# Row tiles for every projection: two 64-row array tiles that take turns on two PSUM banks, in a fixed instruction order, with x held in SBUF

## The chip, the cores, the metric

One core of a Trainium2 chip runs the whole program. The metric is the device time of one execution in microseconds; medians of several executions are given. A profiled execution has a *span* (first to last instruction); the measured time is 1.7 to 2.1 us longer than the span here.

## The reference

A transformer block of 2048 tokens and width 576: layer norm, linear attention with 32 heads of 18, and a gated GELU network of width 4608, both on the normalized x, both added to x. All data are bf16.

```python
def reference(x, wqkv, wo, w_gate, w_up, w_down):          # cut to what matters
    xn = layernorm(x)                                      # 2048 x 576
    q, k, v = split_heads(xn @ wqkv)                       # 32 heads of 18
    phi = lambda t: where(t > 0, t + 1, exp(t)) + 1e-6
    pq, pk = phi(q), phi(k)
    kv, z = einsum(pk, v), sum_over_tokens(pk)
    o = (pq @ kv) / (pq . z + 1e-6)
    return x + o @ wo + (gelu(xn @ w_gate) * (xn @ w_up)) @ w_down
```

The width 576 is 4 x 128 + 64. Each projection therefore contracts over four full chunks of 128 rows and one chunk of 64 rows; what to do with the half chunk is the subject of the change.

## The kernel before

The stages follow each other: for each tile of 128 tokens layer norm, transposes and the K and V projections with the products of phi(K) and V ("K/V stage"); then Q; then, four times (for 512 tokens each), gate/up followed by the down projection. TensorE's products go to *PSUM tiles* of one bank here and two in the changed kernel, which are reused in turn: a product waits until the last reader of its tile is done. Three engines work on phi: ScalarE makes relu(-t) and then exp, VectorE max(t, 0) + eps, GpSimd adds the two. phi_e and phi_a are the buffers between them. The *denominators* are the products pq . z (`ps_den`).

```python
    def phi(ps_ap, out_ap, rows, cols, add_eng):
        e = awork.tile([P, SC], F32, name="phi_e", tag="phi_e")
        nc.scalar.activation(out=e[...], in_=ps_ap, func=ACT.Relu, scale=-1.0)
        nc.scalar.activation(out=e[...], in_=e[...], func=ACT.Exp, scale=-1.0)
        a = awork.tile([P, SC], F32, name="phi_a", tag="phi_a")
        nc.vector.tensor_scalar(out=a[...], in0=ps_ap, scalar1=0.0, scalar2=EPS_ATT, op0=ALU.max, op1=ALU.add)
        add_eng.tensor_tensor(out=out_ap, in0=e[...], in1=a[...], op=ALU.add)

    # K, V, Q: five full-array products per output; the fifth chunk of the weights is padded with zeros
            for kt in range(KT):
                nc.tensor.matmul(ps_k[:, :HALF], lhsT=xnT[:, kt, ts_], rhs=wqkv_sb[:, kt, ...],
                                 start=(kt == 0), stop=(kt == KT - 1))

    # gate and up: four full-array products each, then the two half chunks as one pair of 64-row tiles
        def full(self, first):
            ...
                        nc.tensor.matmul(pst[:], lhsT=wsb[:, kt, fcol], rhs=xnT[:, kt, self.cs], ...)
        def pairs(self, first):
            for i in range(self.r):
                nc.tensor.matmul(self.g[i][:], lhsT=self.wr[0:64, fcol], rhs=xnT[0:64, 4, self.cs], ...)
                nc.tensor.matmul(self.u[i][:], lhsT=self.wr[64:128, fcol], rhs=xnT[64:128, 4, self.cs], ...)
    # ... two batches in a row, the second in the order pairs, full: one change of tiling mode in, one out
    # ... denominators of the first 512 tokens: in the first five double batches of gate/up
    # ... Q: every third add of phi on VectorE, the others on GpSimd
    # ... each down tile loads its x again for the last addition
```

The order of instructions on each engine was left to a scheduler.

## Time and profile before

The time was 544.41 us (median of 3). Read from the timeline of TensorE:

| | before |
|---|---|
| first K matmul | 10.94 us |
| K of two tiles to K of the next two | 6.02 us |
| Q starts | 63.22 |
| gate/up starts (from Q's start) | 84.82 (21.60) |
| gate/up stages, from first to last slot | 74.49, then three of 71.85; sum 290.04 |
| span | 542.6 |

A *slot* is the time from one start on TensorE to the next. With 512 columns it is 216 ns, whether one full-array product or two 64-row products side by side fill it. In the page, "PE 528.8 (97%)" is time in which TensorE had work; it does not say that each slot did as much as it could.

### The profile page before, as it was taken

The numbers are of one execution on the slowest core, as the hardware profiler recorded it, in microseconds if no ns is written. First come the engines' busy times: TensorE is split into PE (matmuls) and PEld (weight loads), VectorE is DVE, ScalarE is ACT, GpSimd is POOL, SyncE is SP. The second block draws the span as 40 slices with busy tenths as digits, with TensorE's granted clock in tenths as the row PEclk, the third lists the DMA queues.
The fourth block names the chain that finished last, engine by engine and source line by source line (L and its number), as shares of the span: only waits on it lengthen the run. The fifth ranks groups of instructions, "written<-read, shape, count | busy, mean of one in ns | idle before, by whom it ended". The sixth has DMA issues, their size and how long they took to land.

```text
span 542.6 us, 8817 instructions
## 1 busy us (share of the span) xinstructions
PE 528.8 (97%) x3371; PEld 311.4 (57%) x3403; DVE 258.0 (48%) x462; ACT 152.0 (28%) x329; POOL 67.8 (12%) x79
## 2 busy tenths in 40 slices
PE   5999999999999999999999999999999999999997
PEld 4788764444457774444477744444677644445775
DVE  5996598877248613333288123323683123323101
ACT  3677797223330003223200013223100122322000
POOL 1445465101002100000011000000021000000000
PEclk8999999999999999999999999999999999999999
DMA  8920003897840114554511035545301245540000
GB/s 251 251 78 2 1 2 95 254 257 211 227 135 24 29 34 141 155 145 143 163 52 38 28 103 145 161 137 154 110 23 32 74 136 157 148 127 0 23 18 16
DMA packets 104851, 58.08 MB, mean 107 GB/s; under 512 B 5802, under 2 KB 104746, under 8 KB 104810
## 3 DMA queue, kind: packets, MB, share of 16 engines
q1 hardware_dynamic: 104810, 57.53, 37.6%
q8 instruction: 26, 0.43, 0.4%
q14 instruction: 15, 0.12, 0.1%
HBM read 55.15 MB, written 2.36 MB: 106 GB/s over the span
## 4 chain that ended last, share of the span: by engine, by line
PE 92%; DMA 2%; DVE 2%; SPq 1%; issue 1%; POOL 0%; ACT 0%; POOLq 0%; ACTq 0%
PE acc L468 26%; PE g L392 23%; PE u L392 23%; PE g L400 6%; PE ps_q L332 4%; PE acc L475 4%; DMA xg<-in_A_x_dram 2%; PE ps_k L242 2%; PE ps_v L256 2%; PE ps_den L365 1%; DVE stats L216 1%; DVE phi_a L206 1%; SPq L150 0%; PE tp_x L233 0%; DVE xn L223 0%
## 5 line engine op out<-in xcount | busy, mean ns | idle before, releaser
L409 DVE TENSOR_TENSOR hT<-u,gl 128x512 bf16<-128x512 f32 x144 | 95.7, 686 | 171.9 <-PE u L402 104.2
L408 ACT ACTIVATE gl<-g 128x512 f32<-128x512 f32 x144 | 81.9, 596 | 321.3 <-PE u L402 262.2
L468 PE MATMUL acc<-wd_sb,hT 128*128 128x288 bf16 x1152 | 146.4, 286 | 0.0
L468 PEld LDWEIGHTS <-hT 128*128 128x128 bf16 x1152 | 112.6, 98 | 30.0
L370 DVE RECIPROCAL den_sb<-den_sb 126x128 f32<-126x128 f32 (+3 forms) x100 | 68.0, 746 | 0.7
L371 POOL TENSOR_TENSOR pqT<-pqT,den_sb 126x512 bf16<-126x512 bf16 (+1 forms) x20 | 23.2, 1161 | 298.4 <-DVE den_sb L370 298.4
L480 DVE TENSOR_TENSOR res<-acc,xres 128x288 bf16<-128x288 f32 x32 | 14.6, 457 | 88.3 <-PE acc L475 88.3
L392 PE MATMUL u<-xnT,wu_133 128*128 128x512 bf16 x144 | 37.0, 379 | 0.1
L392 PE MATMUL u<-xnT,wu_131 128*128 128x512 bf16 x144 | 37.0, 379 | 0.1
L392 PE MATMUL u<-xnT,wu_130 128*128 128x512 bf16 x140 | 36.6, 379 | 0.3
L392 PE MATMUL g<-xnT,wg_128 128*128 128x512 bf16 x139 | 36.5, 379 | 0.2
L392 PE MATMUL g<-xnT,wg_127 128*128 128x512 bf16 x136 | 36.0, 380 | 0.7 <-issue 0.5
L392 PE MATMUL u<-xnT,wu_132 128*128 128x512 bf16 x140 | 36.4, 379 | 0.2
L392 PE MATMUL g<-xnT,wg_129 128*128 128x512 bf16 x137 | 36.1, 380 | 0.5 <-issue 0.3
L392 PE MATMUL g<-xnT,wg_126 128*128 128x512 bf16 x140 | 36.4, 379 | 0.1
L242 PE MATMUL ps_k<-wqkv_sb,xnT 128*128 128x288 bf16 x160 | 24.4, 304 | 6.0 <-DVE xnT L234 5.7
L204 ACT ACTIVATE phi_e<-phi_e 128x288 f32<-128x288 f32 (+2 forms) x52 | 26.7, 514 | 1.5
L475 PE MATMUL acc<-m_sb,pqT 126*128 126x288 bf16 (+1 forms) x160 | 24.9, 285 | 0.0
L392 PEld LDWEIGHTS <-wg_127 128*128 128x128 bf16 x144 | 12.6, 98 | 20.7 <-issue 7.9
L392 PEld LDWEIGHTS <-wg_129 128*128 128x128 bf16 x144 | 12.6, 98 | 20.4 <-issue 7.6
L392 PEld LDWEIGHTS <-wu_130 128*128 128x128 bf16 x144 | 14.1, 98 | 17.0
L392 PEld LDWEIGHTS <-wu_131 128*128 128x128 bf16 x144 | 14.1, 98 | 17.0
(96 smaller groups left out, 504.6 us busy)
## 6 DMA issues: line engine op xcount, KB each, us to landing
wd_sb<-in_B_w_down_dram SPq DMA_DIRECT2D x12, 432.0 KB, 4.0
wg_126<-in_B_w_gate_dram SPq DMA_DIRECT2D x18, 256.0 KB, 3.0
wu_130<-in_B_w_up_dram SPq DMA_DIRECT2D x18, 256.0 KB, 4.0
wg_127<-in_B_w_gate_dram SPq DMA_DIRECT2D x18, 256.0 KB, 3.0
wu_131<-in_B_w_up_dram SPq DMA_DIRECT2D x18, 256.0 KB, 3.3
wg_128<-in_B_w_gate_dram SPq DMA_DIRECT2D x18, 256.0 KB, 3.0
wu_132<-in_B_w_up_dram SPq DMA_DIRECT2D x18, 256.0 KB, 3.5
wg_129<-in_B_w_gate_dram SPq DMA_DIRECT2D x18, 256.0 KB, 3.1
```

The lines of the kernel that those rows point to most:

```text
L204: nc.scalar.activation(out=e[:rows, :cols], in_=e[:rows, :cols], func=ACT.Exp, scale=-1.0)
L242: nc.tensor.matmul(ps_k[:, :HALF], lhsT=xnT[:, kt, ts_], rhs=wqkv_sb[:, kt, D + hf * HALF: D + (hf + 1) * HALF], start=(kt == 0), stop=(kt ...
L332: nc.tensor.matmul(ps[:rows, :], lhsT=wqkv_sb[:, kt, q0:q0 + rows], rhs=xnT[:, kt, sc * SC:(sc + 1) * SC], start=(kt == 0), stop=(kt == KT ...
L370: nc.vector.reciprocal(out=dsb[:rows, q * w:(q + 1) * w], in_=dsb[:rows, q * w:(q + 1) * w])
L371: nc.gpsimd.tensor_tensor(out=pqT[:rows, c, cs], in0=pqT[:rows, c, cs], in1=dsb[:rows, :], op=ALU.mult)
L392: nc.tensor.matmul(pst[:], lhsT=wsb[:, kt, fcol], rhs=xnT[:, kt, self.cs], start=(first and kt == 0), stop=(not first and kt == 3),)
L400: nc.tensor.matmul(self.g[i][:], lhsT=self.wr[0:64, fcol], rhs=xnT[0:64, 4, self.cs], start=first, stop=not first)
L408: nc.scalar.activation(out=gl[:], in_=self.g[i][:], func=ACT.Gelu_apprx_tanh)
L409: nc.vector.tensor_tensor(out=hT[:, self.f0 + i, :], in0=self.u[i][:], in1=gl[:], op=ALU.mult)
L468: nc.tensor.matmul(a_ps[:, :HALF], lhsT=hT[:, f, j * P:(j + 1) * P], rhs=wd_sb[:, f, hf * HALF:(hf + 1) * HALF], start=(f == 0), stop=False,)
L475: nc.tensor.matmul(a_ps[:, :HALF], lhsT=pqT[:rows, c, ts_], rhs=m_sb[:rows, c, hf * HALF:(hf + 1) * HALF], start=False, stop=(c == NCH - 1),)
L480: nc.vector.tensor_tensor(out=res[:, hf * HALF:(hf + 1) * HALF], in0=a_ps[:, :HALF], in1=xres[:, hf * HALF:(hf + 1) * HALF], op=ALU.add,)
```

## The change

The intent: where 64-row products go in pairs, a slot holds two halves of anything, so the 18 half chunks of two outputs fill nine slots without padding and without changing the tiling mode. The kernel never lets two row tiles write one bank at the same time (the rule that the prediction cites), so the low rows begin with output 0 and the high rows with output 1 (first phase, five slots), and then they trade banks (second phase, four slots). Between the phases each must know that the other has finished with the bank: an empty instruction on SyncE's queue waits for the end of the first phase, and the second phase waits for it. In the diff this is the *turn*.

```diff
+        def p1(self):
+            for kt in (4, 0, 1, 2, 3):
+                self.mm(0, LO, kt, kt == 4, False)
+                last = self.mm(1, HI, kt, kt == 4, False)
+            self.turn = nc.sync.nop()
+            tc.add_manual_dep(self.turn.ins, last.ins.name, SYNC, reason="the row tiles take turns on a bank")
+
+        def p2(self):
+            for kt in range(4):
+                m = self.mm(1, LO, kt, False, kt == 3)
+                if kt == 0:
+                    tc.add_manual_dep(m.ins, self.turn.ins.name, SYNC, reason="the bank's other row tile has written")
+                self.mm(0, HI, kt, False, kt == 3)
...   K, V, Q, gate and up all use these units; the zero padding goes
+    ctx.enter_context(tc.manual_schedule())
+    x_sb = persist.tile([P, NS, D], BF16, name="x_sb")
...   phi on two banks at once (576 or 1024 columns), all adds on GpSimd:
+            e = awork.tile([P, 2 * SC], F32, name="phi_e", tag="phi_e", bufs=3)
+            a = awork.tile([P, 2 * SC], F32, name="phi_a", tag="phi_a", bufs=2)
...   one round of the K/V stage, in program order:
+        if more:
+            ln_norm(n + 2)
+            ln_norm(n + 3)
+        ka, kb = project_pair(n, "k")
+        fa, fb = k_phi(n, ka), k_phi(n + 1, kb)
+        fa.read()
+        fb.read()
+        if more:
+            tp = transposes([n + 2, n + 3])
+            tp_copy(tp, 0, n + 2, nc.vector.tensor_copy)
+            tp_copy(tp, 1, n + 3, nc.scalar.copy)
...
+        fa.finish()
+        fb.finish()
...
+        va, vb = project_pair(n, "v")
...   the denominators of the first 512 tokens move ahead of gate/up:
+    kv_stage2()
+    den0 = [(c_, den_mm(0, c_)) for c_ in ([0, 1], [2, 3], [4])]
...
-            nc.sync.dma_start(xres[:], x_view[:, n, :])
```

## The prediction

> **What bounds the kernel now.** I read the page first (busy shares, chain of waits), then what TensorE waits for, then its timeline inside the gate/up stage, then the groups of the engines beside it.
>
> ```profile
> span 542.6 us, 8817 instructions
> PE 528.8 (97%) x3371; PEld 311.4 (57%) x3403; DVE 258.0 (48%) x462; ACT 152.0 (28%) x329; POOL 67.8 (12%) x79
> PE 92%; DMA 2%; DVE 2%; SPq 1%; issue 1%; POOL 0%; ACT 0%; POOLq 0%; ACTq 0%
> ```
>
> TensorE is busy 97% and carries 92% of the chain that ended last. So only two things can win time: fewer TensorE slots, or the 14 us in which it idles. The view of waits says where it idles:
>
> ```profile
> PE warm L96 <- POOL ident masks.py:199: 1.8, 1, 1.8
> PE ps_k L242 <- DVE xnT L234: 5.7, 2, 4.4
> ```
>
> The idle time is the start: the first K matmul starts at 10.94 us (timeline), 4.4 us of it because VectorE computed the statistics of tiles 2 and 3, whose load landed at 7.94, before it copied the transposes of tiles 0 and 1. Next the timeline of TensorE in the gate/up stage:
>
> ```profile
> 203.47 1.03 PE L392 MATMUL u<-xnT,wu_132 128*128 128x512 bf16 x4
> 204.42 0.39 PE L400 MATMUL g<-xnT,wr_136 64*128 64x512 bf16 x1
> 204.43 0.39 PE L402 MATMUL u<-xnT,wr_136 64*128 64x512 bf16 x1
> 204.65 0.38 PE L400 MATMUL g<-xnT,wr_136 64*128 64x512 bf16 x1
> 204.87 0.38 PE L400 MATMUL g<-xnT,wr_137 64*128 64x512 bf16 x1
> 205.08 0.38 PE L400 MATMUL g<-xnT,wr_137 64*128 64x512 bf16 x1
> 205.39 1.04 PE L392 MATMUL g<-xnT,wg_129 128*128 128x512 bf16 x4
> ```
>
> Starts are what count here. Full-array matmuls of 512 columns start every 216 ns, those of 288 columns every 122 ns (medians of the starts). The 64-row pairs start together, 3 ns apart, and the next pair follows after 216: two half matmuls cost one slot. But into the pairs it takes 312 ns and out again 312, and the first pair takes 227: 96 + 96 + 11 = 203 ns lost, in each of 36 double batches.
>
> **What the Trainium skill says.**
> - "TensorEngine Tiling (Array Packing)", Key Properties: changing the tiling mode drains TensorE, changing the tile does not. The trace agrees: the 203 ns above.
> - The same page, Gotcha 1: two row tiles may not use one PSUM bank at once, and software must see to it. Nothing in the trace before shows it (g and u pairs have their own banks); it is why the new kernel needs a wait at each change of turns.
> - "SBUF — State Buffer", Who interferes with whom: VectorE in a 2-port mode and GpSimd lock each other out for a whole instruction. The trace agrees: the 64-column normalization takes 0.29 us alone and 0.78 beside GpSimd, and once the 576-column one took 0.78 instead of 0.42.
>
> ```profile
> 20.60 0.29 DVE L227 TENSOR_SCALAR xn<-xg,mv,rstd 128x64 bf16<-128x64 bf16 x1
> 21.93 1.67 POOL L209 TENSOR_TENSOR pk_171<-phi_e,phi_a 128x288 bf16<-128x288 f32 x2 [3.48 <-DVE mv L218]
> 22.85 0.78 DVE L227 TENSOR_SCALAR xn<-xg,mv,rstd 128x64 bf16<-128x64 bf16 x1
> ```
>
> **The change, part by part.** I go through the stages in order.
>
> *Start.* Statistics, normalization, transposes and copy of tile 0 now come before anything of tile 2. First tile landed at about 3.3 us (3.08 before; now the K weights load beside it): two statistics, aggregate, two small activations, normalization, transposes, copy, then the same for tile 1 (durations 0.43, 0.2, 0.29 + 0.2, 0.43, 0.5, 0.45) give the first K matmul at about 7, the second tile's at 8.8, the first K pair done near 10.3, and the norms of tiles 2 and 3 at 11.9. Gain on the start alone about 3 us.
>
> *K/V stage.* Before: two tiles take 6.02 us (K of one tile starts 3.01 after the last), all of it TensorE. TensorE's part falls: 36 slots of 122 ns instead of 40, plus 0.56 transposes and 0.56 for the kv products, plus two mode changes, makes 5.7. But the order is now fixed, and I find a longer loop through the other engines. From phi's max on VectorE, times worked out by scaling the rows before to the new widths (VectorE 288 to 512 columns: 449 to 682 ns, so 576: 0.75, next start after 0.68; ScalarE relu 402 to 587, so 0.64; exp 0.68):
> two max instructions 1.36; first xnT copy 0.48; then the second xnT copy, on ScalarE, which in the built program waits for VectorE's copy of the same PSUM tile, 0.65; the first exp behind it in ScalarE's queue, 0.68: 3.2 us. Then GpSimd adds twice 576 columns:
>
> ```profile
> L209 POOL TENSOR_TENSOR pqT<-phi_e,phi_a 126x512 bf16<-126x512 f32 x11 | 13.8, 1271 | 9.6 <-DVE phi_a L206 4.4 <-ACT phi_e L204 3.9 <-ACT phi_e L203 1.3
> L209 POOL TENSOR_TENSOR pk_171<-phi_e,phi_a 128x288 bf16<-128x288 f32 x8 | 6.3, 795 | 7.6 <-DVE mv L218 4.9 <-DVE phi_a L206 2.7
> ```
>
> (1271 - 795) / 224 = 2.12 ns a column, so 1.40 each, until 6.0. Meanwhile ScalarE does exp, a V copy, Ln, Exp, so the rstd is there at 4.95. Norm, copy, norm, copy need 1.5: without the lock the next max starts at 6.45, with the lock they end about 1.3 after GpSimd, at 7.3. Either is over 6.02, so this stage becomes slower although TensorE has less to do. With 7.3: norms of tiles 14 and 15 at 11.9 + 6 x 7.3 = 55.7. After that come the rest of its group and the last K pair (6.1), then 4.95 until GpSimd has made the last pk and the last kv product ran. The Q stage starts at 66.7 (lock) or 61.6 (no lock), against 63.2 before.
>
> *Q stage.* TensorE: 10 units of 9 slots, 19.4 us instead of 21.6. But before, every third add was on VectorE; now all are on GpSimd: 1024 columns at 2.12 ns and the same fixed part, 2.35 us a unit against 1.94 of TensorE. phi_a has two buffers, so the max of unit i waits for the add of unit i-2. First add at 5.4, max of unit 9 done at 25.4. The three denominator products, now placed before gate/up, take the PSUM tiles of units 7, 8 and 9: TensorE waits at each and reaches gate/up 25.8 us after the start of Q. Without these waits it would be 20.9: 4.9 us lost. Gate/up so starts at 92.5 (lock) or 87.4, against 84.8 before.
>
> *Gate/up and down.* 144 units of 9 slots of 216 are 279.9 us, as before (8 full slots and one pair each). 36 x 203 ns = 7.3 go; 4 entries and exits, 0.8, come. Turn waits: TensorE to SyncE and back I put at 0.15 to 0.25 us (measured: matmul end to other engines 37 to 107 ns, back to TensorE 55); at 512 columns another unit's 864 or 1080 ns lie between, at 288 columns 490, of which 164 go for the matmul's own end. All hidden. SyncE also issues two loads per unit (0.38 + 0.55 before) but those come ahead of the turn's end. Five denominator products and the transposes (1.4 us) have moved ahead of this stage. The m products now open the first down stage, some 0.3 us of waiting. Down: 1312 slots of 122.5 ns, untouched, as is the tail of 3.3.
> Sum from gate/up's start to the end: 279.9 + 0.8 + 1.5 (m) + 3.3 (denominators) + 160.8 + 3.3 = 449.6, and 0.7 that the same sum misses of the 457.8 before: 450.3.
>
> *x in SBUF.* Removes 16 loads of 147 KB; none was on the chain there. Nothing.
>
> **Sum.** With the lock 92.5 + 450.3 = 542.8 of span; without 537.7. The measured time is 1.8 above the span (544.4 against 542.6): 544.6 or 539.5. I weigh the lock two to one: 543.
>
> **Rivals.**
> 1. The loops don't bite: the K/V stage runs at TensorE's 5.75 us per pair and the Q stage hands over without waiting. Then Q starts near 57, gate/up at 78: span about 528, time 530. For it: the intent is plain, and the start and the 6.5 us of mode changes are real. Against it: the fixed order and the buffer counts, read from the program's own waits, and GpSimd's rate, which is measured.
> 2. A long run in 64-row mode doesn't hold 216 ns a slot. Only four pairs in a row were seen; now 36 instructions go into 1944 ns. Each 5 ns more is 1296 x 5 = 6.5 us, to 550. Against it: full 288-column slots issue two instructions every 122 ns, and 133-column ones every 58 (kv products), so issue is no limit at 54 ns, and the weight loads of the next pair started right with the matmuls of the one before.
> 3. SyncE's queue delays the turns: while w_down loads, a turn's end stands behind loads that wait for their own slots. Then TensorE would lose some tenths per block in the first 18 blocks: 2 to 5 us.
>
> **Range and chances.** The two stages with side loops are worth up to 13 us against the best case, and I am less sure of the K/V loop (a few tenths per group times 7) than of GpSimd's backlog in Q. To be faster by over 2% (533.5) both must be mostly wrong: 0.15. Slower by over 2% (555.3) needs rival 2 or 3 at size: 0.05. Range 533 to 551.
>
> **What would show it.** Right: no gap of 312 ns within a gate/up stage, pairs every 216; K pairs 6.5 to 7.5 us apart with VectorE's norms stretched under GpSimd's adds; GpSimd's 1024-column adds back to back at 2.3 us; TensorE waiting some 5 us in all for VectorE's phi_a ahead of the denominator products; gate/up starting later than 84.8. Wrong: K pairs under 6 us apart (loop or lock misread), Q to gate/up within 22 us (adds faster than 2 us), slots of 220 or more, or waits of TensorE for SyncE.

## The result

The changed kernel took 548.3 us (548.06 to 549.0, 4 runs) against 544.47 for the kernel before (544.19 to 545.38, 4 runs): ratio 1.007, 95% interval 1.0056 to 1.0084. By the interval it is a little slower. All outputs are right. The page of the changed kernel:

```profile
span 546.8 us, 11385 instructions
PE 527.7 (97%) x4891; PEld 310.7 (57%) x4891; DVE 247.4 (45%) x378; ACT 148.7 (27%) x247; POOL 71.9 (13%) x66
PEclk8999997999999999999999999999999999999999
PE 82%; DVE 5%; ACT 4%; POOL 3%; issue 3%; SPq 2%; DMA 1%; ACTq 0%; DVEq 0%; POOLq 0%
```

TensorE is still busy 97%, but in the chain of waits it fell from 92% to 82%: VectorE, ScalarE and GpSimd now carry 12% where they carried 2%. The third line is the granted clock in 40 slices: a 7 in the seventh slice (82 to 96 us) stands out. The view of what TensorE waits for (total us, number of times, longest):

```profile
PE tp_x L276 <- DVE xn L264: 4.9, 4, 1.4
PE ps_den L481 <- DVE phi_a L235: 4.1, 3, 1.7
PE ps_k L204 <- ACT v L301: 1.9, 5, 0.4
PE gu L204 <- SPq L213: 0.9, 6, 0.2
```

Before, the only large entry was K waiting at the start. Now there are transposes that wait for a norm, the denominator products that wait for VectorE's phi_a, K products that wait for ScalarE's copy of V, and gate/up products that wait for SyncE. The starts by stage, from the timeline of TensorE:

| | before | after | difference to before, cumulative |
|---|---|---|---|
| first K matmul | 10.94 | 8.85 | -2.1 |
| K pair to K pair | 6.02 | 6.81 | |
| Q starts | 63.22 | 64.60 | +1.4 |
| gate/up starts (from Q's start) | 84.82 (21.60) | 90.86 (26.26) | +6.0 |
| four gate/up stages | 290.04 | 285.32 (72.52, 70.70, 70.99, 71.11) | |
| span | 542.6 | 546.8 | +4.1 |

So the time came in at two places ahead of gate/up, and gate/up gave back less than its mode changes were worth. Each of the three places can be seen.

*A round of the K/V stage in the changed kernel*, from the timeline of all engines (start us, duration us, engine, line, operation; in brackets the idle time before it and what ended that):

```profile
43.44 2.77 POOL L241 TENSOR_TENSOR pk<-phi_e,phi_a 128x576 bf16<-128x576 f32 x2 [4.04 <-ACT phi_e L240]
43.84 0.63 ACT L301 CAST v<-ps_v 128x576 bf16<-128x576 f32 x1
44.52 1.77 PE L204 MATMUL ps_k<-wqkv_sb,xnT 64*128 64x288 bf16 x26 [0.39 <-ACT v L301]
44.69 0.20 ACT L260 ACTIVATE rstd<-rstd 128x2 f32<-128x2 f32 x1
44.93 1.45 DVE L264 TENSOR_SCALAR xn<-x_sb,mv,rstd 128x576 bf16<-128x576 bf16 x1 [0.98 <-ACT rstd L260]
46.51 0.42 DVE L264 TENSOR_SCALAR xn<-x_sb,mv,rstd 128x576 bf16<-128x576 bf16 x1
47.06 1.42 DVE L235 TENSOR_SCALAR phi_a<-ps_k 128x576 f32<-128x576 f32 x2
...
48.39 0.48 DVE L280 COPY xnT<-tp_x 128x640 bf16<-128x640 bf16 x1
48.90 0.69 ACT L280 COPY xnT<-tp_x 128x640 bf16<-128x640 bf16 x1 [1.82 <-DVE xnT L280]
49.49 1.26 ACT L240 ACTIVATE phi_e<-phi_e 128x576 f32<-128x576 f32 x2
```

The same norm takes 1.45 us at 44.93 and 0.42 at 46.51. GpSimd's two adds run from 43.44 to 46.21; the long norm ends at 46.38, 0.17 later. Then follow max, VectorE's copy, ScalarE's copy (which waited 1.82 us for VectorE's), and only then the two exps, which hold back the next adds and the next copy of V.

*From Q to gate/up in the changed kernel*, the timeline of TensorE:

```profile
85.71 0.59 PE L481 MATMUL ps_den<-pqT,zrep 126*126 126x512 bf16 x2 [1.06 <-DVE phi_a L235]
88.03 1.01 PE L481 MATMUL ps_den<-pqT,zrep 126*126 126x512 bf16 x2 [1.73 <-DVE phi_a L235]
90.34 0.59 PE L481 MATMUL ps_den<-pqT,zrep 72*72 72x512 bf16 x1 [1.30 <-DVE phi_a L235]
90.86 0.61 PE L204 MATMUL gu<-xnT,wr 64*128 64x512 bf16 x2
91.26 0.63 PE L204 MATMUL gu<-xnT,wg 64*128 64x512 bf16 x1
91.69 0.63 PE L204 MATMUL gu<-xnT,wg 64*128 64x512 bf16 x1
```

Three waits, and then gate/up begins with starts 427 ns apart instead of 216: the array was at half clock. In gate/up that lasts for nine slots. The trace's record of the granted clock falls from 1.0 to 0.5 at 87.8 us, inside the second wait, and rises again at 94.6: the products at 88.03 are slow already (1.01 us for two, 0.59 at 85.71).

*The first block of a gate/up stage in the changed kernel*, the timeline of all engines again:

```profile
319.77 0.33 SPq L574 DMA_DIRECT2D out_dram<-res  x1
...
321.89 0.51 SPq L168 DMA_DIRECT2D wr<-in_B_w_up_dram  x1
321.98 0.38 PE L204 MATMUL gu<-xnT,wg 64*128 64x512 bf16 x1
322.51 0.39 PE L204 MATMUL gu<-xnT,wu 64*128 64x512 bf16 x1 [0.15 <-SPq L213]
```

The second phase of the block's second unit starts 531 ns after the slot before it instead of 216 (that of the first unit, at 321.32, was 482 after). In SyncE's queue the store of the last output and four load issues stood in front of the turn; the last issue ended at 322.40, and the turn came 0.1 after it. In most later blocks the slots are 216 apart; in this stage one more pair of such waits follows, at 372.27 and 373.46, after a load issue of 1.53 us.

### The profile page after: what moved, and what is told of

Its sections match the earlier page's. It is cut to its first block, busy times and chain, and to the rows that moved or that the text cites. A ratio compares the mean times of both kernels' runs of the same rounds, so it can differ in the third digit from the quotient of the medians.

```text
span 546.8 us, 11385 instructions
## 1 busy us (share of the span) xinstructions
PE 527.7 (97%) x4891; PEld 310.7 (57%) x4891; DVE 247.4 (45%) x378; ACT 148.7 (27%) x247; POOL 71.9 (13%) x66
## 3 DMA queue, kind: packets, MB, share of 16 engines
HBM read 52.86 MB, written 2.36 MB: 101 GB/s over the span
## 4 chain that ended last, share of the span: by engine, by line
PE 82%; DVE 5%; ACT 4%; POOL 3%; issue 3%; SPq 2%; DMA 1%; ACTq 0%; DVEq 0%; POOLq 0%
PE gu L204 50%; PE acc L557 26%; PE acc L563 4%; POOL pqT L241 2%; DVE xn L264 2%; ACT phi_e L240 2%; DVE phi_a L235 1%; PE ps_k L204 1%; ACT xnT L280 1%; DMA x_sb<-in_A_x_dram 1%; PE ps_den L481 1%; ACT v L301 1%; SPq L165 1%; PE ps_q L204 1%; SPq L167 1%
## 5 line engine op out<-in xcount | busy, mean ns | idle before, releaser
L204 PE MATMUL gu<-xnT,wu 64*128 64x512 bf16 x1152 | 275.3, 378 | 1.4 <-SPq L213 0.9
L204 PE MATMUL gu<-xnT,wg 64*128 64x512 bf16 x1152 | 275.7, 378 | 0.0
L543 DVE TENSOR_TENSOR hT<-gu,gl 128x512 bf16<-128x512 f32 x144 | 99.5, 691 | 170.3 <-ACT gl L542 170.3
L542 ACT ACTIVATE gl<-gu 128x512 f32<-128x512 f32 x144 | 86.0, 597 | 322.4 <-PE gu L204 300.5
L204 PEld LDWEIGHTS <-wu 64*128 64x128 bf16 x1152 | 107.3, 94 | 73.6 <-SPq L213 9.7
L204 PEld LDWEIGHTS <-wg 64*128 64x128 bf16 x1152 | 107.3, 94 | 69.0 <-issue 2.0
L493 DVE RECIPROCAL den_sb<-den_sb 126x128 f32<-126x128 f32 (+1 forms) x80 | 67.5, 906 | 0.3
L494 POOL TENSOR_TENSOR pqT<-pqT,den_sb 126x512 bf16<-126x512 bf16 (+3 forms) x25 | 24.1, 965 | 299.5 <-DVE den_sb L493 299.5
L204 PE MATMUL gu<-xnT,wr 64*128 64x512 bf16 x288 | 55.1, 380 | 0.0
L204 PEld LDWEIGHTS <-xnT 64*128 64x128 bf16 x576 | 28.9, 96 | 10.3 <-issue 2.9
```

Of the source, the lines that this page charges most:

```text
L204: return nc.tensor.matmul(self.outs[i], lhsT=self.lhs(i, rows, kt), rhs=self.rhs(i, rows, kt), start=start, stop=stop, skip_group_check=True,)
L493: nc.vector.reciprocal(out=d[:, h:h + P], in_=d[:, h:h + P])
L494: nc.gpsimd.tensor_tensor(out=pqT[:rows, c, cols], in0=pqT[:rows, c, cols], in1=d, op=ALU.mult)
L542: nc.scalar.activation(out=gl[:], in_=ps[:, 0, :], func=ACT.Gelu_apprx_tanh)
L543: nc.vector.tensor_tensor(out=hT[:, GUB * k + i, :], in0=ps[:, 1, :], in1=gl[:], op=ALU.mult)
```

## The experiments

The theory: the products in row tiles cost what was foreseen, and the time is lost in three waits that the new fixed order makes: (1) in the K/V stage a loop through VectorE, ScalarE and GpSimd, lengthened by a lock between VectorE's norm and GpSimd's add; (2) ahead of gate/up an in-order wait for PSUM tiles behind GpSimd's backlog; (3) turns behind other work in SyncE's queue. The main rival: the tiling itself costs something, in slots or in turns. Ratios below are to the kernel before; the changed kernel has 1.007 (548.3 us).

| run | ratio to before (95% interval) | median us | before in the same rounds |
|---|---|---|---|
| e1 adds held, 3 buffers | 1.0094 (1.0066 to 1.0122) | 550.48 | 544.81 |
| e2 exps first | 0.9917 (0.9889 to 0.9945) | 540.57 | 544.81 |
| e3 denominators late | 0.9955 (0.9927 to 0.9982) | 542.78 | 544.81 |
| e4 turns on ScalarE | 0.9996 (0.9973 to 1.0019) | 544.87 | 544.81 |
| e5 adds held, 4 buffers | 1.0006 (0.9981 to 1.0031) | 544.59 | 544.57 |
| e6 gate/up as before | 1.0128 (1.01 to 1.0157) | 551.11 | 544.57 |
| e7 a third phi_a | 1.0044 (1.0018 to 1.0069) | 546.75 | 544.57 |
| e8 all three | 0.9779 (0.975 to 0.9808) | 532.64 | 544.57 |
| e9 K/V on the full array | 1.0079 (1.006 to 1.0098) | 548.18 | 543.96 |
| e10 x loaded again | 1.0081 (1.0066 to 1.0096) | 548.37 | 543.96 |
| e11 e8 and a quicker start | 0.9778 (0.9763 to 0.9792) | 531.77 | 543.96 |
| e12 e1 once more | one run | 549.92 | 543.96 |

### e1 and e12: adds held until the norms are done, three buffers

```diff
         if more:
             ln_norm(n + 2)
-            ln_norm(n + 3)
+            normed = ln_norm(n + 3)
+            for f in held:
+                f.add(normed)        # GpSimd's adds of the last group wait for this norm
...
-            a = awork.tile([P, 2 * SC], F32, name="phi_a", tag="phi_a", bufs=2)
+            ...                      # every third one in a buffer of the denominators, so three in all
```

> The K/V loop alone: GpSimd's two adds of a group are held until VectorE has normalized the next two tiles (phi_a gets a third buffer), so that no add runs beside a norm; nothing else moves. Changed kernel: K pairs start 6.81 us apart, the first norm of a group takes 1.45 us, Q starts at 64.60. Theory A (the lock between the norm and GpSimd's add stretches the loop by 1.03 us per group): norms all 0.42, K pairs 5.75 to 5.95 apart, Q starts at 57.5 to 59, time 541 to 542.5. Rival B (the norm is late because rstd or x or ScalarE is late; the lock only fills a gap): K pairs stay within 6.6 to 6.9, time 547.5 to 549.

Its timed runs took 550.1 to 550.5 us, 2 us more than the changed kernel: neither theory's number. Its profiled execution took 1112 us, and the page of e1 shows why it can't serve:

```profile
span 1110.5 us, 11362 instructions
L204 PE MATMUL gu<-xnT,wg 64*128 64x512 bf16 x1152 | 568.7, 677 | 0.0
```

A gate/up product takes 677 ns instead of 378 throughout, and most of the slots are 440 ns instead of 216, while ScalarE's gelu takes its usual 598 (597 in the changed kernel): TensorE alone was at half speed, from start to end (two times 546 would be 1093). So the run was repeated.

> The first try of held adds once more, for one profile at full clock, since the first one ran at half clock throughout. It took 550.5 in the three other runs, 2 us more than the changed kernel, although no norm can run beside an add in it. Theory A (three buffers: the second relu and max of a group wait until the held add has freed theirs, which puts GpSimd into the loop): norms 0.42, a wait of ScalarE or VectorE for GpSimd in each group, K pairs 6.9 to 7.2. Rival B (something outside the K/V stage): K pairs under 6.6 and the loss elsewhere.

In the second profile (549.92 us, beside 550.1 to 550.5 of e1's timed runs) the norms take 0.43 us each, so the lock is gone, but K pairs are 7.49 to 7.52 us apart, and the view of TensorE's waits of e12 has a new first entry:

```profile
PE ps_v L204 <- DVE phi_a L241: 5.4, 5, 1.5
```

Products of V wait for a PSUM tile that VectorE's max has not read yet. Why it has not is in the timeline of e12, a round of it:

```profile
48.82 2.77 POOL L253 TENSOR_TENSOR pk<-phi_e,phi_a 128x576 bf16<-128x576 f32 x2 [4.76 <-PE ps_k L204]
...
50.27 0.65 ACT L240 ACTIVATE phi_e<-ps_k 128x576 f32<-128x576 f32 x1 [1.19 <-POOL pk L253]
50.95 0.76 DVE L241 TENSOR_SCALAR phi_a<-ps_k 128x576 f32<-128x576 f32 x1 [1.09 <-ACT phi_e L240]
```

The second relu waits 1.19 us for the first held add, whose buffer it takes, and the max comes after the relu. Theory A of this run holds, with a size (7.5) above its range (6.9 to 7.2). The experiment had put GpSimd back into the loop through the buffers, so as a test of the lock it is void. That led to e5.

### e5: adds held, with buffers enough

The same as e1, with four phi_e and four phi_a in the K/V stage and the old buffers in Q.

```diff
+            i = len(phis) % 4 if len(phis) < NS else 0
+            e = d_tile() if i == 3 else awork.tile(..., tag="phi_e", bufs=3)
+            a = d_tile() if i >= 2 else awork.tile(..., tag="phi_a", bufs=2)
```

> The lock by itself, again: the adds of a group held until the next two norms are done, but now with four phi_e and four phi_a buffers in the K/V stage (the spare ones are those of the denominators, idle until Q is over), so that holding the adds makes no later instruction wait for a buffer, as it may have done in the first try, whose only profile ran at half clock and could not tell. Order of ScalarE as in the changed kernel. Theory A (lock): norms 0.42 us, K pairs 5.75 to 6.0 apart as with the exps first, Q starts at 57 to 58.5, time 540 to 542. Rival B (what helped with the exps first was the order on ScalarE, not the absence of the lock): K pairs 6.5 to 6.9, time 546 to 549.

K pairs are 6.33 to 6.34 us apart (6.81 with the lock), Q starts at 60.97 (64.60), the time is 544.59. It lies between the two theories. A round of e5, from the timeline of all engines:

```profile
41.84 1.77 PE L204 MATMUL ps_k<-wqkv_sb,xnT 64*128 64x288 bf16 x26 [0.40 <-ACT v L317]
42.25 0.43 DVE L279 TENSOR_SCALAR xn<-x_sb,mv,rstd 128x576 bf16<-128x576 bf16 x1 [0.98 <-ACT rstd L275]
```

The norm takes 0.43. So the lock is real, but its 1.03 us on the norm are only 0.47 on the round, because a second loop closes at 6.34: the K products at 41.84 wait for ScalarE's copy of V out of the PSUM tile that they need. That copy stands behind the two exps in ScalarE's queue, the exps behind a copy of xnT, and that behind VectorE's copy and both max instructions, which need the K products of this round.

### e2: the exps first

```diff
         fa.read()
         fb.read()
+        fa.finish()                  # exp on ScalarE, add on GpSimd
+        fb.finish()
         if more:
             tp = transposes([n + 2, n + 3])
...
-        fa.finish()
-        fb.finish()
```

> The K/V loop alone, by order instead of by a wait: the two exps on ScalarE and the two adds on GpSimd come before the transposes' copies, so the adds begin about 0.8 us earlier in a group and should end at or before the rstd of the next tiles. Theory A (lock, reached because the exps stand behind a copy that waits for VectorE's copy): norms 0.42 to 0.6, K pairs 5.8 to 6.2 apart, time 541 to 544. Rival B (the copies of the transposes, now 1.4 us later on ScalarE, become the loop): K pairs 6.6 to 7.2 apart, time 547 to 551.

K pairs are 5.80 to 5.81 apart, Q starts at 57.38, the time is 540.57, just under theory A's range. From the timeline of e2:

```profile
38.68 2.38 PE L204 MATMUL ps_k<-wqkv_sb,xnT 64*128 64x288 bf16 x36
...
41.75 1.25 ACT L240 ACTIVATE phi_e<-phi_e 128x576 f32<-128x576 f32 x2
42.52 2.77 POOL L241 TENSOR_TENSOR pk<-phi_e,phi_a 128x576 bf16<-128x576 f32 x2 [3.04 <-ACT phi_e L240]
...
43.28 0.69 ACT L280 COPY xnT<-tp_x 128x640 bf16<-128x640 bf16 x1 [0.28 <-DVE xnT L280]
```

The exps follow the relus at once, the adds end at 45.29, and all sixteen norms average 0.43 us (0.81 in the changed kernel). ScalarE reaches the copy when VectorE is nearly done with its own and waits 0.28 us instead of 1.82. TensorE now waits for nothing in the steady rounds (the K products of the first line have no wait): 5.8 is its own work, and neither loop is the bound. Of the 1.00 us per round, e5 gives 0.47 to the lock; by subtraction 0.53 are left to the loop through the copy of V. (The time fell by 8.2 us on the span; 7.2 of it stand at Q's start. Another 1.0 is in gate/up, 284.31 against 285.32: turn waits, which vary from run to run.)

### e9: the K/V stage on the full array again

```diff
-        a.p1()
-        pb, b = kv_unit(n + 1, which)
-        b.p1()
-        a.p2()
-        b.p2()
+        a.full()                     # five full-array products per output, fifth chunk padded with zeros
+        pb, b = kv_unit(n + 1, which)
+        b.full()
```

> Undoes the row tiles in the K/V stage alone: 20 full-array products a tile and matrix instead of 18 slots of row pairs, the fifth chunk padded with zeros, no turns and no mode changes; order, buffers, Q and gate/up as in the changed kernel. TensorE's own work per pair of tiles then rises from about 5.8 to about 6.2 us. Theory A (the K/V loop runs through VectorE, ScalarE and GpSimd at 6.81 us, so what the tiling saves there buys nothing): K pairs 6.75 to 6.95 apart, time 547.5 to 549.5. Rival B (TensorE's products are part of the loop): K pairs 7.2 to 7.4, time 551 to 553.

K pairs stay at 6.80 to 6.82 and the time at 548.18: in the order of the changed kernel the tiling saves nothing in this stage, as theory A has it. What it saves on TensorE becomes time in which TensorE waits. (What the row tiles are worth here once the loops are gone was not tested by itself.)

### e3: the denominators late

```diff
-    kv_stage2()
-    den0 = [(c_, den_mm(0, c_)) for c_ in ([0, 1], [2, 3], [4])]
+    # in gate/up of the first 512 tokens:
+            if sc == 0 and k in (1, 2, 3):
+                c_ = ([0, 1], [2, 3], [4])[k - 1]
+                d = den_mm(0, c_)
+            elif sc == 0 and k == 5:
+                kv_stage2()
```

> The hand-over from Q to gate/up alone: the three denominator products of the first 512 tokens and the five transposes of kv move from ahead of gate/up into its blocks 1, 2, 3 and 5, so TensorE does not wait for a PSUM tile of the last Q units before it starts gate/up. Changed kernel: Q start to gate/up start 26.26 us, TensorE idle about 6 us in it, and the first nine slots of gate/up at 427 ns instead of 216 (1.9 us). Theory A (in-order wait on PSUM tiles behind GpSimd's backlog): Q to gate/up 20.5 to 22.5 us, no slots of 427, time 541 to 544. Rival B (the backlog holds the PSUM tiles that gate/up takes next, so the wait only moves into its first blocks): the waits reappear as TensorE gu waiting for VectorE phi_a in the first two blocks, time 546 to 548.

Q to gate/up takes 19.48 us instead of 26.26, a little less than the 20.5 to 22.5 expected, and the time is 542.78. From the timeline of e3's TensorE:

```profile
83.97 0.38 PE L204 MATMUL gu<-xnT,wr 64*128 64x512 bf16 x2
84.18 0.38 PE L204 MATMUL gu<-xnT,wg 64*128 64x512 bf16 x1
84.40 0.38 PE L204 MATMUL gu<-xnT,wg 64*128 64x512 bf16 x1
```

The slots are 216 from the first on, and the granted clock is 1.0 from 84 to 94 us: without the idle time the clock stays up. The first gate/up stage grows from 72.52 to 74.00: it now holds the products that moved, and lost the half clock. A rest of rival B is there too: gate/up waits 1.0 us for VectorE's phi_a in two places.

### e7: a third phi_a buffer

```diff
-            a = awork.tile([P, 2 * SC], F32, name="phi_a", tag="phi_a", bufs=2)
+            ...                      # two of these, and every third one in a buffer of the denominators
```

> A third phi_a buffer alone (one of the denominators' in every third unit), order untouched: each max waits for the add three units back instead of two. Theory A (the backlog of GpSimd reaches TensorE through the buffers): the wait ahead of the denominators falls by about one add, 2.35 us, Q to gate/up 23.5 to 24.5 us instead of 26.26, K pairs unchanged at 6.81, time 545 to 546.5. Rival B (the number of buffers is not what holds the PSUM tiles): no change, 548 to 549.

Q to gate/up takes 24.80 us, 1.46 less; 2.35 were expected. The time is 546.75. In the trace of the changed kernel the max of a late unit waits for the add two units back, while its relu had long been done; with the third buffer the relu waits for the add three units back (phi_e has three, too), and the max comes after the relu: one add of 2.35 won, one relu of 1.0 in series again. The mechanism holds; its size, and the time just above the range, were off by the relu.

### e4: gate/up's turns on ScalarE's queue

```diff
-            self.turn = nc.sync.nop()
+            self.turn = (eng or nc.sync).nop()
...
-            u.p1()
+            u.p1(nc.scalar)
```

> The turn waits of gate/up alone: the empty instruction that hands a bank from one row tile to the other stands in ScalarE's queue instead of SyncE's; K/V and Q keep SyncE. Theory A (the 3 to 3.5 us of excess in gate/up come from turns that stand behind stores and load issues in SyncE's queue): no TensorE wait for SyncE in the gate/up stages, each stage 69.9 to 70.4 us from its first slot to the first down slot less the half-clock part, time 544.5 to 546. Rival B (the excess belongs to the tiling: the switch of turns itself costs): stages stay at 70.8 to 71.2 and the time at 548. Rival C (the turn now stands behind a gelu of 0.6 us, so the waits only change their engine): TensorE waits for ScalarE instead, time 548 to 555.

The waits of gate/up for SyncE are gone, the last three stages take 69.94 us each (70.70, 70.99 and 71.11 before the edit), and the time is 544.87. A stage has 36 units of nine slots; at 216 ns that is 69.98, so a stage in row tiles has no excess at all. At the place in a later stage where the changed kernel waited for a turn, the first slot of the second unit's second phase (second line) comes 216 ns after the slot before it:

```profile
320.22 0.38 PE L204 MATMUL gu<-xnT,wu 64*128 64x512 bf16 x1
320.44 0.38 PE L204 MATMUL gu<-xnT,wu 64*128 64x512 bf16 x1
```

All four stages went from 285.32 to 281.75: the turns on SyncE's queue had cost 3.6 us, of which the view of waits named 0.9. The first stage, 71.92, has 1.98 more than the others: that is the half clock.

### e6: gate/up as before

```diff
-            u = _Unit([ps[:, 0, :], ps[:, 1, :]], lhs, ...)
-            u.p1()
...
+        if first:                    # alternating: full array then pairs, pairs then full array
+            full()
+            pairs()
+        else:
+            pairs()
+            full()
```

> Undoes the change in gate/up alone: four full-array products and one 64-row pair again, in alternating order with a mode change between, no turns; K/V, Q, order, x as in the changed kernel. Theory A (203 ns per round of mode changes, 36 rounds, minus 3.5 us of turn waits that go): stages 0.9 us longer than the changed kernel's 71.1 less turn waits of 0.8 each, so about equal to 0.3 longer, time 549 to 552.5 (a change in gate/up worth 1 to 4 us). Rival B (64-row tiles cost something of their own in gate/up, which the turn waits only share): time 545 to 548.

551.11 us. The last three stages take 71.85 us each, to the digit what they take in the kernel before, and with the turns of e4 69.94: the nine rounds of mode changes of a stage cost 1.91 us, 212 ns each (the prediction had 203). Over all four stages (288.76 here, 281.75 in e4, 285.32 in the changed kernel) the change in gate/up is worth 7.0 us without turn waits and 3.4 with them. So rival B, a cost of the tiling itself, falls.

### e10: x loaded again for the last addition

```diff
+        xres = fwork.tile([P, D], BF16, name="xres", bufs=2)
+        nc.sync.dma_start(xres[:], x_view[:, n, :])
...
-                in1=x_sb[:, n, :].rearrange("p (a b) -> p a b", a=2), op=ALU.add)
+                in1=xres[:].rearrange("p (a b) -> p a b", a=2), op=ALU.add)
```

> Undoes the x that stays in SBUF for the last addition: each down tile loads its 128 x 576 of x again, 16 loads on SyncE's queue as before. Theory A (no load of x was on the chain; keeping it buys nothing): 547.5 to 549.0, HBM read 2.3 MB more. Rival B (16 more issues on SyncE's queue stand in front of turns at the start of each gate/up stage): TensorE waits for SyncE grow by 0.5 to 1.5 us, 549 to 550.

548.37 us; HBM read is 55.22 MB instead of 52.86. Keeping x saves bytes and no time. The waits for SyncE did not grow (0.6 us in 4 places, and the four stages sum to 284.67).

### e8: all three remedies

The edits of e2, e3 and e4 together, with a fourth phi_e and phi_a buffer.

> All three remedies at once: exps first, denominators late, turns of gate/up on ScalarE, and a fourth phi_e and phi_a buffer. The three alone gave 8.3, 6.2 and 4.0 us against the changed kernel at 548.3 (by the ratios, 0.9917, 0.9955 and 0.9996 against 1.007). If they act in separate stages they add: 529.5 to 531.5, K pairs 5.8, Q to gate/up 19 to 20.5, stages 70.0; that is 2.5% below the kernel before. If the half clock ahead of gate/up was counted twice, or GpSimd's backlog, now reached 7 us earlier, makes a new wait in gate/up's first blocks: 532 to 536.

532.64 us, 2.2% less than the kernel before and about 15.7 less than the changed kernel: the second of the two ranges expected, so the gains did not quite add. K pairs are 5.76 apart in the steady rounds, Q to gate/up 19.48, the last three stages 69.94, and no slice of the clock is low. The three single gains came to 17.7 us of span (8.2, 5.9, 3.6), the three together to 15.7. Two parts of the difference can be named: 1.0 us of e2's gain were turn waits that also count in e4, and Q starts 0.6 later than in e2, after a first K round of 7.36 instead of 6.74. (That round goes with the clock: its record rises from 0.5 to 1.0 at 13.75 us in e8, at 12.11 in e2.) A 0.7 wait of gate/up for ScalarE's queue, once, is new; the 1.0 wait of e3 for phi_a is gone. The rest of 0.7 or so I did not follow.

### e11: and a quicker start

```diff
     load_x(0, 1, nc.sync)
+    load_x(1, 1, nc.scalar)
     load_w_main(D, 2 * D, nc.scalar)
-    load_x(1, 1, nc.sync)
...
-    ln_half(1, 0, stats1)
     ln_norm(0)
+    ln_half(1, 0, stats1)
```

> The version with all three remedies and, on top, a quicker start: the second tile of x is loaded on ScalarE's queue ahead of the weights, and the norm of the first tile no longer stands behind the second tile's statistics in VectorE's queue. In the changed kernel VectorE waited 0.8 us for that second load before it normalized the first tile. Theory A: first K matmul at 7.9 to 8.4 instead of 9.19, time 531 to 532 (532.64 without it). Rival B (the weights of K, now issued behind x, become the wait): first K matmul stays at 9, time 532.5 to 533.

The first K matmul starts at 8.54 instead of 9.19, less than expected, and the span falls by 0.6 us. The ratio, 0.9778 against 0.9779, can't tell the two apart. What remains at the start is the order on TensorE: tile 0 is copied at 7.17, but the transposes of tile 1, ready at 7.90, stand ahead of K.

## Why the prediction was right, point by point

The time was 548.3 against 543 predicted, within the range of 533 to 551. The side was wrong, though: 543 is a little faster than the kernel before, 548.3 a little slower. The case that held, the one with the lock, had a span of 542.8; it was 546.8: gate/up started 1.6 us earlier than predicted (90.86 against 92.5), and the rest took 5.6 longer. The two errors partly cancel. The term that was mis-sized is the stretch from gate/up's start to the end: 450.3 predicted, 455.9 measured. Two causes make up the 5.6.

- **Start.** K was to start at 7 and started at 8.85. The step that failed is the landing of the second tile of x: it came at 5.74, after the K weights had been issued beside it, and VectorE took that tile's statistics before the first tile's norm. The transposes of tile 1 also stood ahead of K. The gain against before was 2.1 us, not 3. The first K pair, put near 10.3, was done at 12.9: by the trace's record the clock was at half from 9.3 to 12.7 us, and the pair took 4.1 us, where later ones take 2.4.
- **K/V loop, with the lock.** 7.3 predicted, 6.81 measured; Q at 66.7 predicted, 64.60 measured. That there is a loop longer than TensorE's work and that the lock is in it is shown by e2 and e5. The size failed at one step: the norms and copies after the adds' end were put at 1.3 us, and they took 0.85 (47.06 less 46.21), since only the first norm is caught. Q came only 2.1 earlier than predicted because the stretch from the last two norms to Q took 12.9 (51.74 to 64.60), not 11.1.
- **K/V loop, without the lock.** 6.45 predicted, 6.34 measured in e5, but by another loop. The predicted one, from the max through rstd to the norms, would take 5.9: its first part ran 4.68 (44.93 + 6.81 - 47.06) and the two norms with copies 1.2 (e5). What holds e5 at 6.34 is the PSUM tile of V. The number was right by luck.
- **TensorE's own work.** 5.7 predicted for a pair of tiles; 5.76 to 5.81 measured once the loops were gone. e9 shows that the tiling had bought nothing here until then.
- **Q to gate/up.** 25.8 predicted, 26.26 measured; adds 2.35 predicted, 2.38 measured. The waits at the denominators were 4.1 us, 4.9 predicted.
- **Mode changes.** 203 ns a round predicted, 212 by e6 and e4. Less entries and exits, 6.5 us predicted; from gate/up's start to the end e4 and e6 differ by 6.3 (452.4 and 458.8).
- **Rival 2 (slots over 216).** Did not happen: stages of 69.94 leave no room for it.
- **Turn waits.** "All hidden" is the first step that failed. They cost 3.6 us (e4). That another unit's slots hide a turn with nothing in front of it was right (e4 has no excess); but a turn waits in a queue, and "SyncE also issues two loads per unit ... but those come ahead of the turn's end" did not hold where the store of the last output stood first, or where one issue took 1.5 to 1.7 us instead of 0.5. Rival 3 had named the mechanism and put it in the wrong place ("while w_down loads"): it is at the start of the later stages as well. Among the prediction's own signs of being wrong were "waits of TensorE for SyncE", and they came (0.9 us in the view).
- **Half clock.** Was not in the sum: 1.98 us (e4's first stage against its others; gone in e3). Together with the turn waits 5.6, the whole of the miss.
- **x in SBUF.** Nothing predicted, nothing measured (e10).
- **Readings.** Two small ones in the kernel before are off, and nothing hangs on them: products of kv start 61 ns apart by the median, not 58, and the 576-column norm was stretched twice (0.78 us at 17.84, 0.82 at 42.29), not once.

Set against before: the start gained 2.1 us, the K/V loop gave back 3.5 by Q's start, the hand-over to gate/up lost 4.7, and everything after gate/up's start gained 1.9, where gate/up in row tiles without turn waits is worth 7.0 (e6 against e4). So the gain of the tiling was not missing from TensorE: the new order, and all adds on GpSimd, turned it into waits, and e8 gets it back. Left untested are every third add of Q on VectorE as in the kernel before, and the row tiles in an order left to the scheduler.

## What to carry to other kernels

When a change gives TensorE less work, first look for the loop through the other engines that becomes the bound: follow each engine's queue in its new order and ask what each instruction stands behind, above all an instruction that another stage needs (here exps behind a copy that waits for another engine's copy). An empty instruction used as a signal costs its place in the queue, not its duration, so it belongs on a queue where nothing slow stands in front. Products that wait for a late buffer should not stand in front of a long stage that could run without them, and a wait of a few microseconds there can cost again through the clock.

## What the Trainium skill lacked or had wrong

- "TensorEngine Tiling (Array Packing)", Key Properties, says that a mode change drains TensorE and gives no cost. Here a round (into the 64-row pairs and out) cost 203 ns by the starts in the kernel before and 212 ns by the stages of e6 and e4, at 512 columns. A change of tile within the mode cost nothing: 36 units in 69.94 us are 216 ns a slot. Its Gotcha 1 leaves it to software to keep row tiles off one bank, and does not say what the hand-over costs. On SyncE's queue it cost 3.6 us over 144 units; on ScalarE's nothing that e4's stages show, and one wait of 0.7 us in e8.
- "SBUF — State Buffer", Who interferes with whom, calls the lock exclusive for a whole instruction. The trace agrees: a norm of 0.42 us took 1.45 and ended 0.17 us after GpSimd's adds did. In this kernel only the first of two norms in a round was caught, so the cost to the round was 0.47 us (e5).
- "TensorE: Matmul & The Clock Gate", The HAM clock gate, has the array fall to half clock after an idle window of about 3.4 us. In the changed kernel no gap was longer than 1.73 us: a gap of 1.06, 0.6 us of products and a gap of 1.73, within which the clock fell at 87.8, were enough. In e7 it was two gaps of 1.58 and 1.72 with 0.6 us of products between, and the clock fell only at 90.2, when gate/up had run for 0.6 us; so the time before the fall need not be all idle. The half clock lasted 6.8 us in the changed kernel and 3.4 in e7. A later section, A second HAM failure mode, does say that frequent short idle times can lower the clock, but gives no length. With 427 ns for a slot of 512 columns at half clock and 216 at full, its figures agree. The page also warns, under Seeing it yourself, that the clock's records are unreliable and that it has been seen stuck low for over 50 us. One execution of e1 had 677 ns a product for all of its 1110 us, with TensorE busy 99%; its page has no row of the clock (nor has that of e11, which ran normally), and the view of cores gives 1.000. Four further executions of the same kernel (e1's timed ones, e12) were normal. So a whole execution can be lost this way, and the record doesn't tell. No run here shows a cause.
